# Sums of weights on VectorE alone, kept products in the gated tiles, attention blocks in pairs beside the products, ten masks added by VectorE, and buffers moved by 128 bytes

## The chip, the cores and the metric

The kernel runs on one core of one Trainium2 chip. The metric is the device time of one execution in microseconds (us), as the median of several runs; less is better.

## The reference

It computes windowed attention over eight heads and feeds its output through a gated two-layer network. All data are float32; the inputs q and k are drawn at random and scaled by 0.6244 and 0.6248 in all.

```python
# B=8, H=8, S=576, D=64; d_model=512, d_ff=2048
scores = np.matmul(q, k.transpose(0, 1, 3, 2)) / np.sqrt(D)
rel = pos[:, None] - pos[None, :]
mask_plain = (rel >= 0) & (rel < 32)                          # heads 0-3
mask_dil = (rel >= 0) & (rel < 128) & (rel % 4 == 0)          # heads 4-7
attn = softmax(np.where(masks, scores, -1e9))
x = (attn @ v) arranged as (4608, 512)
h = x @ w_in                                                  # (4608, 2048)
g = h * np.clip(h + 3.0, 0.0, 6.0) / 6.0
out = g @ w_out                                               # (4608, 512)
```

## The kernel before

**Precision.** A float32 matrix product is made of three faster ones: each operand is split into a high part and a low part (value minus high part), and high by high, high by low and low by high are added up in PSUM, the accumulator memory that TensorE writes. So every operand costs a cast (its high part) and a subtraction (its low part) on one of the other engines.

**First phase (up to about 140 us).** A list of steps written out by hand (`ORDER`) starts the attention of the first 12 blocks, converts the weights and runs the first tokens through both layers.

**Planned phase.** Everything after is recorded with `op(engine, cost, ...)` and `transfer(...)` and put in order, engine by engine, by a list scheduler (`_in_time`), which goes by costs written in the code and by counts of free buffers. Each engine then runs its own list strictly in order. Three kinds of work matter here:

- *Plain steps.* Tokens go in chunks of 384, the hidden dimension in 16 slices of 128. A step is the first layer of one slice of one chunk (12 matmuls, L561 to L563, into one of the two banks `ps_h`), then ReLU on ScalarE (L569), the gate on VectorE (L572), its high part by GpSimd (`gh`, L576), its low part by VectorE (`gl`, L580), and two steps later the second layer (9 matmuls, L622). There are 64 of these steps; the bank `ps_h` is free again when the gate has read it.
- *Attention blocks.* `attend` runs a couple: the scores of one block and the values of the block before last, one after the other on TensorE (L237, L255), with softmax on VectorE and ScalarE. The first 20 blocks of the planned phase go in ten pairs of couples beside the plain steps 29 to 56 (`SPOTS`); the other 18 couples stand beside the products of the two groups, where `BESIDE` says (group, k, turn): how many at once. The mask of a block is either one more matmul of TensorE into the scores' bank (L347; the blocks in `PE_MASKS`) or an addition by VectorE, `add_mask` (L263).
- *Two groups.* Most tokens are computed by a scheme of Strassen and Winograd: seven products of sums of blocks in place of eight of blocks. The sums of weights are made once per pair of slices, by `combine(side, k)`: 8 for `w_in` (side 0), 8 for `w_out` (side 1). Each is two word sums (L662, 128x512: high plus low part of a weight), four half sums (L670, 128x256), the high part on ScalarE (L674) and the remainder (L679, 128x1024); two DMAs then write it to DRAM (`sums`, `rights`), from where a ring of six buffers brings it back, 512 KB a piece. The sums of tokens (`fill`, L751 and L758) are VectorE's too, and GpSimd copies pieces of attention output for them (L471). A group's products of one k are 7 times 6 matmuls (L783 to L785), whose results are kept (`keep`, L1081), added (`add`, L1088) and gated (`gated`, L1040 and L1045); then the second layer follows (`second_products`, L774, fed by L1203, L1234, L1238).

Which engine makes the word sums and the remainder is set by the letters in `BY_POOL`: `w` and `l` name GpSimd, `s` (half sums) is not among them, so that these are VectorE's.

Of the kernel before, what the change touches and what calls it, by code (L numbers as in the profile page):

```python
# [9 lines left out]
F32 = mybir.dt.float32  # L10
F32R = mybir.dt.float32r
# [4 lines left out]
AF = mybir.ActivationFunctionType  # L16
# [24 lines left out]
SPOTS = tuple((m, 1) for m in range(29, 57, 3))  # L41
SPARE = (1, 1, 1, 1, 1, 1, 1, 1), (1, 1, 1, 1, 1, 1, 1, 1)
LEAD_SUMS = 300.0
BY_POOL = ("wl",) * 8, ("wl",) * 8
GAPS = {(0, 0): 2}
LATER = 3
LANDING = 2.6
EARLY = 100.0
PE_MASKS = frozenset(range(24))
SHARED = frozenset(range(16))  # L50
WIPED = {(0, 0)}
BESIDE = {**{(0, k, 0): 1 for k in range(8)}, **{(0, k, 3): 1 for k in (2, 4, 6)}, **{(1, k, 0): 1 for k in range(7)}}
HIGH_BY = ("aaaaaaaa",) * 7

# [33 lines left out]
def windowed_attention_ffn(ctx: ExitStack, tc: tile.TileContext, qk, vp, w, mask, out, out_t):  # L88
# [55 lines left out]
    def wide_tile(name, dtype=F32):  # L144
        return work.tile([P, CG], dtype, name=name, tag="work")
# [14 lines left out]
        return mi[:rows, at : at + CH]  # L160

    ident = const.tile([P, P], F32, name="ident")
    three = const.tile([P, 1], F32, name="three")

# [489 lines left out]
    ]  # L654
    KEPT = (T1, T3, T4, T2, R11, R21, R22)

    def combo_words(side, k, i, eng):

        if (side, k) not in combos:
            combos[side, k] = w_tile("v", [4, HALF])  # L660
        x, v = (win, wout)[side][2 * k + i], combos[side, k]
        eng.tensor_tensor(  # L662
            out=v[:, 2 * i : 2 * i + 2].rearrange("p a n -> p (a n)"), in0=x[:, 0].bitcast(F32), in1=x[:, 1].bitcast(F32), op=ALU.add
        )

    def combo_sum(side, k, i, eng):

        v = combos[side, k]
        to, a, b, op = SUMS[side][i]
        eng.tensor_tensor(out=v[:, to], in0=v[:, a], in1=v[:, b], op=op)  # L670

    def combo_high(side, k):
        hi = w_tile("sh", [4, HALF], F32R)
        nc.scalar.copy(hi, combos[side, k])  # L674
        combos[side, k] = combos[side, k], hi

    def combo_low(side, k, i, n, eng):
        v, hi = (x[:, i * 4 // n : (i + 1) * 4 // n] for x in combos[side, k])
        eng.tensor_tensor(out=v.bitcast(F32R), in0=v, in1=hi.bitcast(F32), op=ALU.subtract)  # L679

    def combo_plain(side, k):
        a, b = ((win, wout)[side][2 * k + i] for i in range(2))
# [253 lines left out]
    words, combined, taken = {}, {}, {}  # L936

    def combine(side, k):
        of = lambda what, n: ("POOL", 0.3 + n * 0.00205, nc.gpsimd) if what in BY_POOL[side][k] else ("DVE", 0.16 + n * 0.00104, nc.vector)
        e, us, eng = of("w", DM)  # L940
        x = op(e, us, lambda: combo_words(side, k, 0, eng), takes=[("w", 2, SPARE[side][k])], ahead=LEAD_SUMS)
        words[side, k] = x = op(e, us, lambda: combo_words(side, k, 1, eng), [x], ahead=EVER)
        e, us, eng2 = of("s", HALF)
        for i in range(4):
            x = op(e, us, lambda i=i: combo_sum(side, k, i, eng2), [x], ahead=EVER)
        x = op("ACT", 1.05, lambda: combo_high(side, k), [x], ahead=EVER)
        e, us, eng3 = of("l", 4 * HALF)
        x = op(e, us, lambda: combo_low(side, k, 0, 1, eng3), [x], ahead=EVER)
        combined[side, k] = [
            transfer(0.9, 2.0, lambda: combo_out(side, k), [x], gives=[("w", 2)]),  # L950
            transfer(1.35, 1.5, lambda: combo_plain(side, k), ahead=EARLY),
        ]
# [83 lines left out]
    kept_gates = {}  # L1036

    def gated(h, after, g, q, k, from_bank):
        r = op(
            "ACT", 0.7, lambda: nc.scalar.activation(gated_tile(g, q, k), h(), AF.Relu, bias=three, scale=1.0),  # L1040
            [after, kept_gates.get((g, q, k - 1)) if k % 2 else None], takes=() if k % 2 else SLOT,
        )
        x = op(
            "DVE", 0.69,
            lambda: nc.vector.scalar_tensor_tensor(  # L1045
                out=gated_tile(g, q, k), in0=gated_tile(g, q, k), scalar=6.0, in1=h(), op0=ALU.min, op1=ALU.mult
            ),
            [r], gives=FREE if from_bank else ONE,
        )
        kept_gates[g, q, k] = x  # L1050
        if from_bank:
            freed.append(x)
# [21 lines left out]
    def products_of(g, k):  # L1074

        at_bank, kept = {}, {}

        def keep(name, after):
            def do():
                kept[name] = wide_tile("s")  # L1080
                nc.scalar.copy(kept[name], at_bank["x"])  # L1081

            return op("ACT", 0.59, do, [after], takes=ONE)

        def add(name, bank, after, gives):
            x = op(
# [57 lines left out]
    def second_products(g):  # L1144
# [75 lines left out]
        def halves(p, k):  # L1220
# [7 lines left out]

            def high_():
                two.append(wide_tile("gh", F32R))  # L1230
                if by_pool:
                    nc.gpsimd.tensor_copy(out=two[0], in_=gated_tile(g, q, k))
                else:
                    nc.scalar.copy(two[0], gated_tile(g, q, k))  # L1234

            def low_():
                two.append(wide_tile("gl", F32R))
                nc.vector.tensor_tensor(out=two[1], in0=gated_tile(g, q, k), in1=two[0].bitcast(F32), op=ALU.subtract)  # L1238

            by_pool = HIGH_BY[p][k] == "p"  # L1240
            x = op("POOL" if by_pool else "ACT", 0.8 if by_pool else 0.62, high_, after, takes=[("work", 1, 5)], ahead=8.0)
            y = op("DVE", 0.69, low_, [x], takes=ONE, gives=gives)
            lows[q, name, k] = y
            return two, [x, y]
# [334 lines left out]
```

## Time and profile before

| | |
|---|---|
| median of 3 runs | 862.13 us (862.04 to 862.76) |
| the profiled execution | 861.62 us, of which the span in the profile is 859.8 us |
| TensorE clock granted, mean over the span | 0.988 of full speed |
| busy, share of the span | PE 834.7 us (97%), VectorE 642.9 us (75%), ScalarE 556.8 us (65%), GpSimd 143.5 us (17%) |
| DMA | 184.94 MB in the span, 215 GB/s on the mean |

All views are of this one profiled execution. PE is TensorE's matmul side, PEld its loading of weights; DVE is VectorE, ACT ScalarE, POOL GpSimd, SP the engine that issues DMAs. Busy shares are means over stages with different limits, so the views by stretch of time tell more than this table.

### The profile page before, as it was taken

To read this page: it belongs to the slowest core of one execution; us is meant where nothing else is said; L and a number is where in the kernel's file an instruction comes from. 1 tells how busy PE (TensorE), PEld (TensorE's weight loads), DVE (VectorE), ACT (ScalarE), POOL (GpSimd) and SP (SyncE) were. 2 spreads that over 40 slices of the span, in tenths; PEclk is the share of its full clock that TensorE was granted. 3 is DMA by queue.
4 is the path that set the end of the run, shared out by engine and by line. 5 is a ranking of instruction groups with operands and counts; after the bars stand their busy time and mean duration, and the time that the engine had idled before them with its cause. 6 is when DMAs were issued, how large, how long until landed. Compare 5 with 4: busy or idle time off the path is not lost.

```text
span 859.8 us, 20361 instructions
## 1 busy us (share of the span) xinstructions
PE 834.7 (97%) x8103; PEld 693.8 (81%) x8103; DVE 642.9 (75%) x1130; ACT 556.8 (65%) x1271; POOL 143.5 (17%) x170
## 2 busy tenths in 40 slices
PE   7999999999999889699999999999999999999998
PEld 4788999888888778577778888877888888888886
DVE  4899996567678998976789997566599844449953
ACT  3688776259989786277997774677565524456542
POOL 0000000235447867640011000001000000000000
PEclk9899999999999999889999999999999999999999
DMA  8746433157667879988778475868446369661441
GB/s 299 260 148 232 123 115 129 42 178 238 199 214 247 290 251 349 308 291 278 263 267 287 164 263 168 278 230 301 160 147 227 125 235 378 233 216 55 177 165 74
DMA packets 99454, 184.94 MB, mean 215 GB/s; under 512 B 6560, under 2 KB 35232, under 8 KB 99360
## 3 DMA queue, kind: packets, MB, share of 16 engines
q1 hardware_dynamic: 99360, 183.65, 62.5%
q8 instruction: 64, 1.05, 0.5%
q14 instruction: 30, 0.25, 0.1%
HBM read 144.83 MB, written 38.80 MB: 214 GB/s over the span
## 4 chain that ended last, share of the span: by engine, by line
PE 85%; DVE 9%; ACT 2%; issue 2%; POOL 1%; DMA 1%; SPq 0%; DVEq 0%; POOLq 0%; ACTq 0%
PE ps_o L774 27%; PE ps_o L622 11%; PE ps_x L783 9%; PE ps_x L785 9%; PE ps_x L784 9%; PE ps_h L561 4%; PE ps_h L562 4%; PE ps_h L563 4%; DVE v L670 2%; DVE gl L580 2%; PE ps_b L255 1%; PE ps_a L237 1%; PE ps_a L247 1%; PE ps_a L364 1%; DVE mx L290 1%
## 5 line engine op out<-in xcount | busy, mean ns | idle before, releaser
L774 PE MATMUL ps_o<-gh,ring 128*128 128x512 f32 x672 | 182.7, 389 | 0.0
L774 PEld LDWEIGHTS ps_o<-gh,ring 128*128 128x128 f32 x672 | 126.1, 188 | 26.5
L1238 DVE TENSOR_TENSOR gl<-g,gh 128x512 fp32r<-128x512 f32 x168 | 108.6, 685 | 23.0 <-ACT gh L1234 17.1
L1234 ACT CAST gh<-g 128x512 fp32r<-128x512 f32 x168 | 98.0, 622 | 37.7 <-PE ps_o L774 35.5
L774 PE MATMUL ps_o<-gl,ring 128*128 128x512 f32 x336 | 103.8, 389 | 0.0
L783 PE MATMUL ps_x<-cells,ring 128*128 128x512 f32 x240 | 97.1, 405 | 0.1
L622 PE MATMUL ps_o<-wo,gh 128*128 128x512 f32 x372 | 97.1, 397 | 0.0
L561 PE MATMUL ps_h<-x,wi 128*128 128x384 f32 x256 | 89.5, 350 | 6.2 <-DVE t L572 3.5
L785 PE MATMUL ps_x<-cells,ring 128*128 128x512 f32 x240 | 95.4, 398 | 0.0
L562 PE MATMUL ps_h<-x,wi 128*128 128x384 f32 x256 | 87.3, 341 | 0.6 <-issue 0.6
L563 PE MATMUL ps_h<-x,wi 128*128 128x384 f32 x256 | 87.5, 342 | 0.0
L622 PEld LDWEIGHTS ps_o<-wo,gh 128*128 128x128 f32 x372 | 70.6, 191 | 11.8
L774 PEld LDWEIGHTS ps_o<-gl,ring 128*128 128x128 f32 x336 | 63.1, 188 | 13.3
L784 PE MATMUL ps_x<-cells,ring 128*128 128x512 f32 x176 | 70.0, 398 | 0.0
L580 DVE TENSOR_TENSOR gl<-t,gh 128x384 fp32r<-128x384 f32 x64 | 58.6, 916 | 10.5 <-POOL gh L576 8.5
L1045 DVE SCALAR_TENSOR_TENSOR g<-g,ps_x 128x512 f32<-128x512 f32 x48 | 32.7, 682 | 44.5 <-ACT g L1040 44.0
L784 PE MATMUL ps_x<-cell,ring 128*128 128x512 f32 x160 | 62.8, 392 | 0.0
L471 POOL COPY raw<-xf 128x96 f32<-128x96 f32 (+8 forms) x56 | 23.8, 474 | 221.2 <-ACT xf L402 217.9
L569 ACT ACTIVATE t<-ps_h,three 128x384 f32<-128x384 f32 x64 | 37.3, 585 | 33.9 <-PE ps_h L563 32.0
L402 ACT COPY a<-a_t 32x192 f32<-32x192 f32 x144 | 50.4, 350 | 11.9 <-DVE a L395 7.7
L1203 DVE TENSOR_TENSOR g<-g 128x1024 f32<-128x1024 f32 x48 | 57.4, 1217 | 0.0
L561 PEld LDWEIGHTS ps_h<-x,wi 128*128 128x128 f32 x256 | 48.4, 189 | 10.2 <-DVE t L572 4.5
(129 smaller groups left out, 1699.7 us busy)
## 6 DMA issues: line engine op xcount, KB each, us to landing
ring<-sums SPq DMA_DIRECT2D x84, 512.0 KB, 6.7
ring<-rights SPq DMA_DIRECT2D x84, 512.0 KB, 4.7
st<-in_w SPq DMA_DIRECT2D x32, 512.0 KB, 3.8
kq<-in_qk SPq DMA_DIRECT2D x39, 416.0 KB, 4.0
v<-in_v SPq DMA_DIRECT2D x39, 390.0 KB, 5.3
sums<-wi SPq DMA_DIRECT2D x24, 256.0 KB, 7.2
rights<-wo SPq DMA_DIRECT2D x24, 256.0 KB, 5.4
out<-o SPq DMA_DIRECT2D x11, 512.0 KB, 3.4
```

What stands on the lines that cost most here:

```text
L561: nc.tensor.matmul(ph, lhsT=wt(f, 0)[:, ks], rhs=a, start=(kt == 0), stop=False)
L562: nc.tensor.matmul(ph, lhsT=wt(f, 0)[:, ks], rhs=b, start=False, stop=False)
L563: ins = nc.tensor.matmul(ph, lhsT=wt(f, 1)[:, ks], rhs=a, start=False, stop=(kt == NK - 1))
L580: return nc.vector.tensor_tensor(out=gls[n], in0=ts.pop(n), in1=ghs[n].bitcast(F32), op=ALU.subtract)
L622: ins = nc.tensor.matmul(po[c][tt], lhsT=g[:, tt * P : (tt + 1) * P], rhs=wt(f, row), start=(f == 0 and not i), stop=(f == NF - 1 and i == 2))
L774: nc.tensor.matmul(banks[part], lhsT=right[:, a, cols], rhs=x, start=(start and not i), stop=(i == 2), skip_group_check=True)
L783: nc.tensor.matmul(bank, lhsT=tile_[:, 0, ks], rhs=h[:, kt], start=(start and kt == 0), stop=False, skip_group_check=True)
L784: nc.tensor.matmul(bank, lhsT=tile_[:, 0, ks], rhs=l[:, kt], start=False, stop=False, skip_group_check=True)
L785: nc.tensor.matmul(bank, lhsT=tile_[:, 1, ks], rhs=h[:, kt], start=False, stop=(kt == 1), skip_group_check=True)
L1203: nc.vector.tensor_tensor(out=at[0], in0=at[1], in1=at[2], op=alu)
L1234: nc.scalar.copy(two[0], gated_tile(g, q, k))
L1238: nc.vector.tensor_tensor(out=two[1], in0=gated_tile(g, q, k), in1=two[0].bitcast(F32), op=ALU.subtract)
```

## The change

It has six parts. (1) `BY_POOL` goes: the 32 word sums and the 16 remainders are VectorE's, as the half sums were. (2) `keep` writes a product into the gated tile of its slice, which lies in the pool of 4 KB slots, in place of a work tile; the ReLU of a kept product writes a work tile in its turn. (3) `BESIDE` puts single couples and pairs beside the products, where there were single ones only: 11 beside the first group and 7 beside the second, as before. (4) Ten blocks (0 to 9 of the planned phase) get their mask from VectorE rather than from TensorE. (5) Two more slices of the first group clear a bank by a matmul (L1105) before a product is copied into it, so that the bank is taken earlier. (6) The tile `three` takes 160 bytes a partition where it took 4, and everything allocated behind it lies 128 bytes higher. `HIGH_BY` named ScalarE throughout; it goes, and nothing is moved by that.

```diff
-BY_POOL = ("wl",) * 8, ("wl",) * 8
-PE_MASKS = frozenset(range(24))
+PE_MASKS = frozenset(range(10, 24))
-WIPED = {(0, 0)}
-BESIDE = {**{(0, k, 0): 1 for k in range(8)}, **{(0, k, 3): 1 for k in (2, 4, 6)}, **{(1, k, 0): 1 for k in range(7)}}
-HIGH_BY = ("aaaaaaaa",) * 7
+WIPED = {(0, 0), (0, 6), (0, 7)}
+BESIDE = {**{(0, k, 0): 1 for k in range(3)}, **{(0, k, 0): 2 for k in range(3, 7)}, (1, 0, 0): 1, **{(1, k, 0): 2 for k in (2, 4, 6)}}
...
-    three = const.tile([P, 1], F32, name="three")
+    three = const.tile([P, 40], F32, name="three")[:, :1]
...
     def combine(side, k):
-        of = lambda what, n: ("POOL", 0.3 + n * 0.00205, nc.gpsimd) if what in BY_POOL[side][k] else ("DVE", 0.16 + n * 0.00104, nc.vector)
-        e, us, eng = of("w", DM)
-        x = op(e, us, lambda: combo_words(side, k, 0, eng), takes=[("w", 2, SPARE[side][k])], ahead=LEAD_SUMS)
-        words[side, k] = x = op(e, us, lambda: combo_words(side, k, 1, eng), [x], ahead=EVER)
-        e, us, eng2 = of("s", HALF)
+        x = op("DVE", 0.69, lambda: combo_words(side, k, 0), takes=[("w", 2, SPARE[side][k])], ahead=LEAD_SUMS)
+        words[side, k] = x = op("DVE", 0.69, lambda: combo_words(side, k, 1), [x], ahead=EVER)
         for i in range(4):
-            x = op(e, us, lambda i=i: combo_sum(side, k, i, eng2), [x], ahead=EVER)
+            x = op("DVE", 0.43, lambda i=i: combo_sum(side, k, i), [x], ahead=EVER)
         x = op("ACT", 1.05, lambda: combo_high(side, k), [x], ahead=EVER)
-        e, us, eng3 = of("l", 4 * HALF)
-        x = op(e, us, lambda: combo_low(side, k, 0, 1, eng3), [x], ahead=EVER)
+        x = op("DVE", 1.22, lambda: combo_low(side, k), [x], ahead=EVER)
...
     def gated(h, after, g, q, k, from_bank):
+        t = {}
+
+        def do():
+            t[0] = gated_tile(g, q, k) if from_bank else wide_tile("t")
+            nc.scalar.activation(t[0], h(), AF.Relu, bias=three, scale=1.0)
...
-                out=gated_tile(g, q, k), in0=gated_tile(g, q, k), scalar=6.0, in1=h(), op0=ALU.min, op1=ALU.mult
+                out=gated_tile(g, q, k), in0=t[0], scalar=6.0, in1=h(), op0=ALU.min, op1=ALU.mult
...
         def keep(name, after):
...
-                kept[name] = wide_tile("s")
+                kept[name] = gated_tile(g, q, k)
                 nc.scalar.copy(kept[name], at_bank["x"])
 
-            return op("ACT", 0.59, do, [after], takes=ONE)
+            return op("ACT", 0.59, do, [after, kept_gates.get((g, q, k - 1)) if k % 2 else None], takes=() if k % 2 else SLOT)
```

The lines of the changed kernel have other numbers: the gate L572 is L570 there, `gl` L580 is L578, a token sum L751 or L758 is L749 or L756, a word sum L662 is L660, a half sum L670 is L668, a remainder L679 is L677, GpSimd's cast L576 is L574 and its copies L471 are L469.

The first place is GpSimd's list around the last casts of gates, up to the cast of the 64th, which is the last L576. Before, sums of weights stand between the casts (`wo` is a weight of the second layer, `v` and `sh` a sum and its high part):

```order
L576 CAST gh<-t 128x384
L662 TENSOR_TENSOR v<-wo 128x512
L679 TENSOR_TENSOR v<-v,sh 128x1024
L576 CAST gh<-t 128x384
L662 TENSOR_TENSOR v<-wo 128x512 x3
L576 CAST gh<-t 128x384 x2
L679 TENSOR_TENSOR v<-v,sh 128x1024 x2
L576 CAST gh<-t 128x384
L679 TENSOR_TENSOR v<-v,sh 128x1024 x2
```

With the change the same stretch of GpSimd's list, up to the same last cast, holds copies of attention output and casts:

```order
L574 CAST gh<-t 128x384
L469 COPY raw<-xf 128x2x48
L469 COPY raws<-xf 128x2x64
L469 COPY raw<-xf 128x2x80
L574 CAST gh<-t 128x384 x6
```

All sums are gone from between the casts; nothing takes their place on GpSimd.

The second place is VectorE's list around the same gates, from the 61st to the low part of the 64th. Before, half sums and token sums (`cells`, `cell`) stand between gate and low part:

```order
L572 SCALAR_TENSOR_TENSOR t<-t,ps_h 128x384
L670 TENSOR_TENSOR v<-v 128x256 x5
L580 TENSOR_TENSOR gl<-t,gh 128x384
L670 TENSOR_TENSOR v<-v 128x256
L572 SCALAR_TENSOR_TENSOR t<-t,ps_h 128x384
L670 TENSOR_TENSOR v<-v 128x256 x2
L580 TENSOR_TENSOR gl<-t,gh 128x384
L670 TENSOR_TENSOR v<-v 128x256 x6
L758 TENSOR_TENSOR cell<-raws,cells 128x1024
L572 SCALAR_TENSOR_TENSOR t<-t,ps_h 128x384
L758 TENSOR_TENSOR cells<-t,cells 128x1024
L580 TENSOR_TENSOR gl<-t,gh 128x384
```

With the change the same stretch reads:

```order
L570 SCALAR_TENSOR_TENSOR t<-t,ps_h 128x384
L756 TENSOR_TENSOR cells<-t,cells 128x1024
L578 TENSOR_TENSOR gl<-t,gh 128x384
L660 TENSOR_TENSOR v<-wo 128x512
L668 TENSOR_TENSOR v<-v 128x256
L660 TENSOR_TENSOR v<-wo 128x512
L570 SCALAR_TENSOR_TENSOR t<-t,ps_h 128x384
L668 TENSOR_TENSOR v<-v 128x256
L677 TENSOR_TENSOR v<-v,sh 128x1024
L578 TENSOR_TENSOR gl<-t,gh 128x384
L668 TENSOR_TENSOR v<-v 128x256 x4
L756 TENSOR_TENSOR cell<-raws,cells 128x1024
```

Word sums and remainders have come between the gates, and half sums have left them: over VectorE's list from the 51st to the 64th gate there are 20 half sums, 10 word sums and 5 remainders where there were 35 half sums. From the 28th to the 51st gate there are 14 word sums, 5 remainders and 10 masks more and 2 half sums fewer; from the 64th gate to the first low part of the second layer (L1238) 8 word sums, 6 remainders and 18 half sums where there was one half sum. These three stretches hold all 32 word sums and 16 remainders.

The third place is VectorE's list beside the first group, where `BESIDE` puts couples (`e` is a score tile with its mask added, `mx` the rows' largest scores, `z` their sums; the numbers tell buffers apart). Before, one couple stood there at a time:

```order
L263 TENSOR_TENSOR e_6153<-ps_b_6092,mi_81 128x384
L322 TENSOR_SCALAR z_6161<-ps_b_6093 128x6
L323 RECIPROCAL z_6161<-z_6161 128x6
L325 TENSOR_TENSOR x_6164<-ps_b_6093,z_6161 128x384
L289 TENSOR_REDUCE mx_6175<-e_6153 128x6
L290 TENSOR_SCALAR mx_6175<-mx_6175 128x6
L1045 SCALAR_TENSOR_TENSOR g_6157<-g_6157,s_5525 128x512
```

With the change, where a pair stands:

```order
L261 TENSOR_TENSOR e_6167<-ps_b_6041,mi_81 128x384
L261 TENSOR_TENSOR e_6174<-ps_a_6091,mi_81 128x384
L287 TENSOR_REDUCE mx_6188<-e_6167 128x6
L288 TENSOR_SCALAR mx_6188<-mx_6188 128x6
L287 TENSOR_REDUCE mx_6193<-e_6174 128x6
L288 TENSOR_SCALAR mx_6193<-mx_6193 128x6
L320 TENSOR_SCALAR z_6204<-ps_a_6092 128x6
L321 RECIPROCAL z_6204<-z_6204 128x6
L323 TENSOR_TENSOR x_6207<-ps_a_6092,z_6204 128x384
```

The masks and maxima of two blocks now stand together, ahead of the next product's gate, where those of one block did.

## Rows read from the trace of the kernel before

**Rows 1.** Windows: us of window, PE, PEld, DVE, ACT, POOL busy (instructions), PEclk, DMA, GB/s.

```profile
166.00:280.00 114.00, 114.00 (x1786) 99.88 (x1788) 80.88 (x178) 93.47 (x300) 56.43 (x65) 1.00 0.63 205
280.00:365.00 85.00, 70.30 (x839) 60.19 (x828) 79.91 (x119) 51.89 (x138) 60.40 (x53) 0.95 0.90 301
280.00:380.00 100.00, 85.28 (x1070) 71.87 (x1059) 91.93 (x134) 61.65 (x161) 68.14 (x57) 0.93 0.89 295
365.00:455.00 90.00, 89.90 (x1371) 70.95 (x1372) 68.94 (x147) 75.39 (x192) 15.11 (x26) 0.97 0.82 275
720.00:740.00 20.00, 20.00 (x88) 16.16 (x87) 7.93 (x12) 9.19 (x16) 0.00 (x0) 1.00 1.05 386
```

**Rows 2.** Waits of PEld, 280 to 380 us: total us, times, longest.

```profile
PEld ps_b L255 <- DVE t L572: 4.7, 1, 4.7
PEld ps_h L561 <- DVE t L572: 4.5, 3, 2.6
PEld ps_h L561 <- ACT e L298: 3.4, 2, 3.2
PEld ps_a L255 <- ACT o L922: 2.5, 1, 2.5
```

**Rows 3.** The chain within 340 to 366 us, by line.

```profile
by line: DVE v L670 27.2%; DVE gl L580 19.0%; DVE cell L758 17.8%; POOL gh L576 13.2%; DVE cells L758 8.5%; issue 8.4%; DVE t L572 7.2%; DVE t L751 4.4%; DVEq L580 0.2%; POOLq L576 0.1%; DVEq L572 0.1%
```

**Rows 4.** VectorE's groups, 280 to 365 us: busy us, mean ns, idle before.

```profile
L580 DVE TENSOR_TENSOR gl<-t,gh 128x384 fp32r<-128x384 f32 x13 | 20.0, 1541 | 1.4 <-POOL gh L576 1.4
L670 DVE TENSOR_TENSOR v<-v 128x256 f32<-128x256 f32 x35 | 19.9, 598 | 0.3
L290 DVE TENSOR_SCALAR mx<-mx 128x6 f32<-128x6 f32 x6 | 7.3, 1213 | 0.2
...
L758 DVE TENSOR_TENSOR cell<-t,cells 128x1024 fp32r<-128x1024 f32 x1 | 3.4, 3405 | 0.0
```

**Rows 5.** VectorE's groups, 60 to 140 us, when GpSimd was idle.

```profile
L580 DVE TENSOR_TENSOR gl<-t,gh 128x384 fp32r<-128x384 f32 x21 | 11.6, 552 | 0.1
...
L545 DVE TENSOR_TENSOR wo<-va,wo 128x512 fp32r<-128x512 f32 x13 | 8.9, 686 | 1.2 <-ACT wo L539 1.1
```

**Rows 6.** GpSimd's groups, 280 to 365 us.

```profile
L662 POOL TENSOR_TENSOR v<-wo 128x512 f32<-128x512 f32 x16 | 23.1, 1458 | 0.0
L679 POOL TENSOR_TENSOR v<-v,sh 128x1024 fp32r<-128x1024 f32 x8 | 20.1, 2521 | 1.1 <-ACT sh L674 1.1
L576 POOL CAST gh<-t 128x384 fp32r<-128x384 f32 x13 | 10.2, 785 | 20.8 <-DVE t L572 20.8
L471 POOL COPY raws<-xf 128x128 f32<-128x128 f32 (+4 forms) x10 | 5.5, 551 | 0.0
L471 POOL COPY raw<-xf 128x160 f32<-128x160 f32 (+3 forms) x6 | 3.7, 610 | 0.0
```

**Rows 7.** Timeline, 304 to 305 us: start us, us.

```profile
304.08 2.38 POOL L679 TENSOR_TENSOR v<-v,sh 128x1024 fp32r<-128x1024 f32 x1
304.25 2.23 DVE L290 TENSOR_SCALAR mx<-mx 128x6 f32<-128x6 f32 x1
```

**Rows 8.** VectorE's groups over the whole span.

```profile
L1203 DVE TENSOR_TENSOR g<-g 128x1024 f32<-128x1024 f32 x48 | 57.4, 1217 | 0.0
...
L263 DVE TENSOR_TENSOR e<-ps_b,mi 128x384 f32<-128x384 f32 x12 | 6.6, 550 | 2.3 <-PE ps_b L237 2.3
```

**Rows 9.** TensorE's timeline around a couple with a mask of TensorE's.

```profile
398.21 0.40 PE L785 MATMUL ps_x<-cells,ring 128*128 128x512 f32 x1
398.44 0.34 PE L347 MATMUL ps_b<-mi 128*128 128x384 bf16 x1
398.71 0.24 PE L255 MATMUL ps_b<-v,a 64*32 64x65 f32 x1
```

**Rows 10.** TensorE's timeline around a couple without such a mask.

```profile
413.73 0.39 PE L785 MATMUL ps_x<-cell,ring 128*128 128x512 f32 x1
414.05 0.24 PE L255 MATMUL ps_b<-v,a 64*32 64x65 f32 x1
```

More of the change, by code (lines that the diff above doesn't have):

```diff
@@ L655, in windowed_attention_ffn, with combo_words @@
     KEPT = (T1, T3, T4, T2, R11, R21, R22)
-    def combo_words(side, k, i, eng):
+    def combo_words(side, k, i):
         if (side, k) not in combos:
@@ L661, in combo_words, with combo_sum @@
         x, v = (win, wout)[side][2 * k + i], combos[side, k]
-        eng.tensor_tensor(
+        nc.vector.tensor_tensor(
             out=v[:, 2 * i : 2 * i + 2].rearrange("p a n -> p (a n)"), in0=x[:, 0].bitcast(F32), in1=x[:, 1].bitcast(F32), op=ALU.add
         )
-    def combo_sum(side, k, i, eng):
+    def combo_sum(side, k, i):
         v = combos[side, k]
         to, a, b, op = SUMS[side][i]
-        eng.tensor_tensor(out=v[:, to], in0=v[:, a], in1=v[:, b], op=op)
+        nc.vector.tensor_tensor(out=v[:, to], in0=v[:, a], in1=v[:, b], op=op)
     def combo_high(side, k):
@@ L675, in combo_high, with combo_low @@
         combos[side, k] = combos[side, k], hi
-    def combo_low(side, k, i, n, eng):
-        v, hi = (x[:, i * 4 // n : (i + 1) * 4 // n] for x in combos[side, k])
-        eng.tensor_tensor(out=v.bitcast(F32R), in0=v, in1=hi.bitcast(F32), op=ALU.subtract)
+    def combo_low(side, k):
+        v, hi = combos[side, k]
+        nc.vector.tensor_tensor(out=v.bitcast(F32R), in0=v, in1=hi.bitcast(F32), op=ALU.subtract)
     def combo_plain(side, k):
@@ L1038, in gated @@
     def gated(h, after, g, q, k, from_bank):
+        t = {}
+        def do():
+            t[0] = gated_tile(g, q, k) if from_bank else wide_tile("t")
+            nc.scalar.activation(t[0], h(), AF.Relu, bias=three, scale=1.0)
         r = op(
-            "ACT", 0.7, lambda: nc.scalar.activation(gated_tile(g, q, k), h(), AF.Relu, bias=three, scale=1.0),
-            [after, kept_gates.get((g, q, k - 1)) if k % 2 else None], takes=() if k % 2 else SLOT,
+            "ACT", 0.7, do, [after, kept_gates.get((g, q, k - 1)) if k % 2 else None],
+            takes=ONE if not from_bank else () if k % 2 else SLOT,
         )
@@ L1078, in keep @@
         def keep(name, after):
+            q = int(name[1:])
             def do():
-                kept[name] = wide_tile("s")
+                kept[name] = gated_tile(g, q, k)
                 nc.scalar.copy(kept[name], at_bank["x"])
-            return op("ACT", 0.59, do, [after], takes=ONE)
+            return op("ACT", 0.59, do, [after, kept_gates.get((g, q, k - 1)) if k % 2 else None], takes=() if k % 2 else SLOT)
         def add(name, bank, after, gives):
@@ L1230, in high_ @@
                 two.append(wide_tile("gh", F32R))
[L1231 to L1234, printed above, removed]
+                nc.scalar.copy(two[0], gated_tile(g, q, k))
             def low_():
@@ L1238, in low_ @@
                 nc.vector.tensor_tensor(out=two[1], in0=gated_tile(g, q, k), in1=two[0].bitcast(F32), op=ALU.subtract)
-            by_pool = HIGH_BY[p][k] == "p"
-            x = op("POOL" if by_pool else "ACT", 0.8 if by_pool else 0.62, high_, after, takes=[("work", 1, 5)], ahead=8.0)
+            x = op("ACT", 0.62, high_, after, takes=[("work", 1, 5)], ahead=8.0)
             y = op("DVE", 0.69, low_, [x], takes=ONE, gives=gives)
```

## The prediction

> **What bounds the kernel now.** The windows view comes first: busy time of each engine by stretch [rows 1]. From 166 to 280 us TensorE's matmul side is busy for 114.00 of 114 us at the full clock, and from 365 to 455 us for 89.90 of 90: there nothing but fewer matmuls shortens the run. Between 280 and 380 us it is busy for 85.28 of 100 us and its granted clock is 0.93. The first is 14.7 us of idleness; the second is 7.0 us more (100 x 0.07), since the matmuls that do run are drawn out when the clock falls to its lower level (1.2 in place of 2.4 GHz) in part of a stretch that has gaps. These 21.7 us are what a better order could give back.
>
> Who holds TensorE up there the list of waits tells [rows 2]: 4.7 and 4.5 us for the gate L572, 3.4 and 2.5 us for the exponentials and for a scaled output on ScalarE, 15.1 us together. Three of the four end at softmax or gate work, which comes off VectorE's list or behind it. The chain of waits from 340 to 366 us names the cause more sharply [rows 3]: half sums L670 27%, low parts L580 19%, token sums L758 26%, gates 7%, all VectorE's, and 13% GpSimd's cast. In the windows VectorE is busy for 79.91 of the 85 us from 280 to 365 [rows 1]. So VectorE is full exactly where TensorE starves.
>
> But is it full of work? In that stretch one L580 takes 1541 ns on the mean, one L670 598, one L290 (128x6 elements!) 1213, one token sum 3405 [rows 4]. From 60 to 140 us, with GpSimd idle, the same L580 takes 552 ns, and a 128x512 addition 686 [rows 5]; a 128x1024 one takes 1217 [rows 8]. From these two a 128x256 half sum would take 0.42 us (0.686 less half of 0.531). The excess is 13 x 0.99 = 12.9 us in L580, 35 x 0.18 = 6.3 in L670, 6 x about 1.0 = 6 in L290 (an estimate: 64 times the elements take 0.55 in L263 [rows 8]), 2.2 in that one L758: some 27 us of records that are blocked, not working. What blocks them is seen in the timeline: GpSimd's remainder starts at 304.08 and lasts 2.38 us, L290 starts at 304.25 and lasts 2.23, both end at 306.46 to 306.48 [rows 7]. GpSimd is busy there for 60.40 us [rows 1], of which word sums and remainders are 23.1 + 20.1 = 43.2 and the casts and copies 19.4 [rows 6].
>
> **Part 1, the sums to VectorE.** *Added work:* 32 word sums at 0.686 us and 16 remainders at 1.217 [rows 5, 8], 22.0 + 19.5 = 41.4 us, with the ten masks at 0.55 (5.5 us) 46.9. By VectorE's order it falls in three places.
> - From the 28th to the 51st gate, about 166 to 280 us: 14 x 0.686 + 5 x 1.217 + 10 x 0.55 - 2 x 0.42 = 20.3 us. VectorE's 80.88 of 114 us [rows 1] become at most 101. It stays hidden behind matmuls that are unbroken now; without that cover it would cost its 20.3 us.
> - From the 51st to the 64th gate: 10 x 0.686 + 5 x 1.217 - 15 x 0.42 = 6.6 us.
> - From the 64th gate to the first low part of the second layer: 8 x 0.686 + 6 x 1.217 + 17 x 0.42 = 19.9 us. VectorE's 68.94 of 90 us [rows 1] become 88.8.
>
> *Removed:* GpSimd's 43.2 us in the starved stretch. VectorE's 91.93 busy us from 280 to 380 hold about 27 of blocking, so 64.5 of work; with 6.6 more 71.1. What GpSimd keeps there, 19.4 us of casts and copies, is 0.32 of its 60.40; if blocking goes with GpSimd's time, 27 x 0.32 = 8.7 us stay: 79.8 us of VectorE against 78.3 of TensorE at the full clock (100 - 21.7). That is 1.5 us over, on par. The bounds of what TensorE still loses there are 0 and today's 14.7. I take 3.5: the 1.5, and 2 for gates whose cast or low part stands behind a 1.2 us sum in a full queue. Beside the first group I take 3.5 as well: 88.8 us in a window of some 88 leaves VectorE no slack, but a few us of the 68.94 were blocking by GpSimd's last remainders. Bounds there: nothing, and the whole 19.9 if VectorE's idle time of before (21 of 90 us) can't be used because results it waits for come late. With gaps this short I let the clock come back whole; a clock that stays low keeps up to 7.0.
>
> By the order, GpSimd's casts now stand behind no sum on their own engine. That shortens the way from gate to low part only where a sum ran when the gate ended: GpSimd was idle for 20.8 us ahead of casts, until their gate came [rows 6]. I count nothing for it beyond the unblocking.
>
> The pair of records at 304 us shows whole instructions waiting for one another [rows 7]. The Trainium skill says why, in "SBUF — State Buffer", section "SBUF: two separate sides": VectorE and GpSimd share a pair of ports, held as an exclusive lock for a whole instruction, and a VectorE operation with two SBUF inputs contends with a GpSimd operation that reads SBUF. The trace agrees for the two-input L580, but the proportional 8.7 us would be too mild by that rule: it is what the third case below prices.
>
> **Part 2, kept products in the gated tiles.** The copies, additions and gates keep their sizes and engines; nothing is added. What changes is which pool they wait for: the 4 KB slots are taken at the copy rather than at the ReLU. In rows of before no wait there names either pool; I take 0, with bounds of 2 us either way.
>
> **Part 3, pairs beside the products.** TensorE's entry into a couple costs 0.32 us from the last product matmul (413.73 to 414.05) where the next matmul otherwise follows after 0.23 (398.21 to 398.44) [rows 9, 10]: 0.09 per entry. Seven couples join another; the way back to the products isn't in these rows, and I take it alike: 0.7 us gained, between 0 and 1.3. In VectorE's list two masks and two maxima now stand ahead of a product's gate, about 1.8 us more delay there (0.55 + 0.55 and smaller ones); six banks for products and scores hide it, and it is in the 3.5 above.
>
> **Part 4, ten masks.** With TensorE's mask the block's first matmul comes 0.50 us after the last product (398.21 to 398.71), without it 0.32 [rows 9, 10]: 0.18 each, 1.8 us gained for ten, in stretches where TensorE is unbroken. Bounds: 0 and 3.4 (ten times the record's 0.34). VectorE's side is counted above.
>
> **Part 5, two wipes:** two 128x512 matmuls at the products' pitch of 0.23, 0.5 us lost. **Part 6, 128 bytes:** no instruction changes its size; I take 0, bounds 2 us either way: DMA's busy share is 0.89 in the starved stretch [rows 1], but none of the waits there ends with a DMA [rows 2].
>
> **The sum**, against the profiled execution's own 861.6 us (span 859.8 and 1.8 around it): - 21.7 - 0.7 - 1.8 + 0.5 + 3.5 + 3.5 = 844.9. The median of the runs lies 0.5 above the profiled one, so 845.4.
>
> **Rivals.**
> - *All stalls go* (VectorE's sums fit between the gates, casts come early): neither 3.5 is paid, 838.4. For it: VectorE would be on par even with blocking that stays. Against: par leaves no room for a bad order.
> - *Half the gain* (each cast and copy blocks VectorE for its whole length): 19.4 in place of 8.7 stay, 10.7 us more on a VectorE that is the bound: 845.4 + 10.7 = 856. For it: the pair of records at 304 us [rows 7]. Against: some casts run while VectorE waits for that very cast (1.4 us idle before L580 [rows 4]), and such a cast blocks nothing.
> - *DMA late.* By the order of SP's list twelve pieces of sums for `w_out`, about 0.52 MB each, move past the 64th gate, into the window that carries 275 GB/s for 90 us = 24.8 MB [rows 1]. About 31 MB in 88 us are 352 GB/s; 386 is the most in any of these windows. If ring pieces come behind these writes, some 10 us: 855. Against: TensorE's waits name no DMA in rows 2.
> - *Slower: VectorE becomes the bound.* If the excess of 27 us isn't GpSimd's sums (it could come with DMA or PSUM traffic), it stays: 91.9 + 6.6 = 98.5 us of VectorE against 78.3, a stall of 20, and its clock loss of 7 stays; beside the first group half of the 19.9, 10 us, come out on the path. 838.4 + 20 + 7 + 10 = 875. It decides from 23.7 us of stalls and clock loss on (21.7 + 0.7 + 1.8 - 0.5). Against: the common end at 306.46, and 552 ns in rows 5 under other DMA and PSUM traffic.
>
> **The numbers.** Forecast (841 to 850): 0.42. All stalls go: 0.20. Half the gain: 0.20. DMA: 0.06. VectorE the bound: 0.12. The range of 8 in 10 leaves out the last and the ends of the others: 836 to 857. About 0.2% (1.7 us) can be told from no change; faster by more 0.86, same 0.03, slower 0.11.
>
> **What would show it.** Right: no L662 or L679 on GpSimd, L580 near 0.6 to 0.8 us and half sums near 0.42 between 280 and 365 us; TensorE busy for over 93 of 100 us there and its clock back near 1.00; waits on gates under 5 us. Wrong: L580 still above 1.2 us (blocking not by the sums); PEld waiting for L1045 or L1091 beside the first group for over 5 us (VectorE full there); waits of products that end with a DMA.

## The result, and the profile after

The changed kernel takes 849.1 us (median of four runs, 847.94 to 849.82) where the kernel before takes 862.44 beside it: a ratio of 0.9838, with an interval of 0.9819 to 0.9856. The profiled execution takes 849.62 us, 12.0 us less than that of before; its span is 847.4 us. A second measurement of the same kernel (`again`, below) gives 0.9821 (0.9794 to 0.9848).

The page's lines for TensorE's and GpSimd's busy time, and for the shares of the chain that ended last:

```profile
PE 827.2 (98%) x8095; PEld 691.7 (82%) x8095; DVE 639.2 (75%) x1188; ACT 557.4 (66%) x1271; POOL 59.3 (7%) x122
...
PE 89%; ACT 4%; DMA 2%; DVE 2%; issue 2%; POOL 0%; SPq 0%; DVEq 0%; ACTq 0%; POOLq 0%
```

VectorE has taken over 41 us of sums and is still busy for 3.7 us less than before (642.9): its records have become shorter. The windows by stretch, columns as in [rows 1]:

```profile
166.00:280.00 114.00, 112.11 (x1914) 99.89 (x1913) 86.72 (x204) 97.56 (x305) 26.20 (x49) 1.00 0.63 205
280.00:380.00 100.00, 99.83 (x1285) 85.58 (x1284) 89.54 (x183) 70.95 (x184) 16.95 (x26) 0.99 0.96 326
342.00:440.00 98.00, 92.43 (x1387) 73.02 (x1386) 82.38 (x181) 79.19 (x196) 10.41 (x26) 0.98 0.90 314
365.00:455.00 90.00, 84.39 (x1169) 66.32 (x1168) 74.12 (x158) 77.97 (x194) 10.20 (x26) 0.98 0.87 309
530.00:620.00 90.00, 88.22 (x825) 70.99 (x824) 57.42 (x108) 60.60 (x133) 4.81 (x14) 0.98 0.64 227
```

The starved stretch is gone: from 280 to 380 us TensorE is busy for 99.83 of 100 us, where it was 85.28 [rows 1]. But it is now idle for 1.9 us ahead of it, 5.6 us beside the first group (365 to 455) and 1.8 us beside the second (530 to 620), and those three were full before (90.00 of 90 us in the last). The first of them isn't new, though. It is the wait for a scaled output at 278 us, and the kernel before has the same wait inside the starved stretch (start, us, line, idle before):

```profile
283.30 0.24 PE L255 MATMUL ps_a<-v,a 64*32 64x65 f32 x1 [2.26 <-ACT o L922]
```

The windows are fixed in time and the work in them has moved ahead, so that this wait has left the stretch without going away. (The trace has three groups of products, not two; couples stand beside the first two, and the third has none.) VectorE's groups from 265 to 350 us, where the last plain steps now run:

```profile
L668 DVE TENSOR_TENSOR v<-v 128x256 f32<-128x256 f32 x28 | 11.9, 446 | 0.2
L578 DVE TENSOR_TENSOR gl<-t,gh 128x384 fp32r<-128x384 f32 x16 | 8.9, 554 | 2.0 <-POOL gh L574 2.0
```

The low part of a gate takes 554 ns where it took 1541, a half sum 446 where it took 598 [rows 4]. The waits of TensorE's matmuls from 160 to 830 us (total us, times, longest):

```profile
PE ps_x L782 <- issue: 3.4, 1, 3.4
PE ps_x L781 <- ACT g L1084: 2.1, 2, 1.5
PE ps_a L253 <- ACT o L920: 1.9, 1, 1.9
PE ps_a L253 <- issue: 1.8, 1, 1.8
PE ps_o L620 <- issue: 0.2, 1, 0.2
```

No wait for a gate is left, and no wait for VectorE at all. Two end with ScalarE: for a scaled output (L920) and for kept copies (L1084). The two longest other ones are called "issue": TensorE waited for nothing that the profile shows. What that is, the experiments had to tell.

### The profile page after: what moved, and what is told of

Same layout as the page of the kernel before. It is cut to its first block, busy times and chain, and to the rows that moved or that the text cites. A ratio compares the mean times of both kernels' runs of the same rounds, so it can differ in the third digit from the quotient of the medians.

```text
span 847.4 us, 20299 instructions
## 1 busy us (share of the span) xinstructions
PE 827.2 (98%) x8095; PEld 691.7 (82%) x8095; DVE 639.2 (75%) x1188; ACT 557.4 (66%) x1271; POOL 59.3 (7%) x122
## 4 chain that ended last, share of the span: by engine, by line
PE 89%; ACT 4%; DMA 2%; DVE 2%; issue 2%; POOL 0%; SPq 0%; DVEq 0%; ACTq 0%; POOLq 0%
PE ps_o L772 27%; PE ps_o L620 14%; PE ps_x L781 9%; PE ps_x L782 8%; PE ps_x L783 8%; PE ps_h L559 5%; PE ps_h L560 5%; PE ps_h L561 5%; PE ps_a L235 2%; PE ps_a L253 2%; DMA kq<-in_qk 1%; PE ps_a L362 1%; PE ps_a L245 1%; PE ps_b L253 1%; ACT a L400 1%
## 5 line engine op out<-in xcount | busy, mean ns | idle before, releaser
L1238 DVE TENSOR_TENSOR gl<-g,gh 128x512 fp32r<-128x512 f32 x168 | 108.8, 687 | 24.7 <-ACT gh L1234 18.3
L620 PE MATMUL ps_o<-wo,gh 128*128 128x512 f32 x372 | 94.6, 390 | 0.2 <-issue 0.2
L782 PE MATMUL ps_x<-cells,ring 128*128 128x512 f32 x176 | 70.3, 399 | 3.4 <-issue 3.4
L782 PE MATMUL ps_x<-cell,ring 128*128 128x512 f32 x160 | 63.6, 397 | 0.0
L1091 DVE TENSOR_TENSOR g<-ps_x,g 128x512 f32<-128x512 f32 x48 | 33.1, 689 | 39.8 <-ACT g L1084 32.7
L783 PEld LDWEIGHTS ps_x<-cells,ring 128*128 128x128 f32 x240 | 45.9, 191 | 14.7 <-issue 3.6
L781 PEld LDWEIGHTS ps_x<-cells,ring 128*128 128x128 f32 x240 | 45.8, 191 | 12.3 <-ACT g L1084 0.8
L620 PE MATMUL ps_o<-wo,gl 128*128 128x512 f32 x186 | 52.2, 389 | 0.0
L400 ACT COPY a<-a_t 32x192 f32<-32x192 f32 x144 | 50.5, 350 | 2.6
```

The lines of the kernel that those rows point to most:

```text
L400: ins = nc.scalar.copy(dst[QB * to : QB * (to + 1), u * CH // 2 : (u + 1) * CH // 2], mid[QB * c : QB * (c + 1), : CH // 2])
L620: ins = nc.tensor.matmul(po[c][tt], lhsT=g[:, tt * P : (tt + 1) * P], rhs=wt(f, row), start=(f == 0 and not i), stop=(f == NF - 1 and i == 2))
L781: nc.tensor.matmul(bank, lhsT=tile_[:, 0, ks], rhs=h[:, kt], start=(start and kt == 0), stop=False, skip_group_check=True)
L782: nc.tensor.matmul(bank, lhsT=tile_[:, 0, ks], rhs=l[:, kt], start=False, stop=False, skip_group_check=True)
L783: nc.tensor.matmul(bank, lhsT=tile_[:, 1, ks], rhs=h[:, kt], start=False, stop=(kt == 1), skip_group_check=True)
```

## The experiments

All of them run the whole computation; only the two with fillings and `shift` add work that nothing uses.

**Is it GpSimd's sums?** Two kernels separate the first part from the rest. `pool_back` is the changed kernel with the sums on GpSimd again:

```diff
 def combo_words(side, k, i):
-        nc.vector.tensor_tensor(
+        nc.gpsimd.tensor_tensor(
 def combo_low(side, k):
-        nc.vector.tensor_tensor(out=v.bitcast(F32R), in0=v, in1=hi.bitcast(F32), op=ALU.subtract)
+        nc.gpsimd.tensor_tensor(out=v.bitcast(F32R), in0=v, in1=hi.bitcast(F32), op=ALU.subtract)
```

with the three operations recorded for GpSimd at the former costs.

> The changed kernel with its 32 word sums and 16 remainders on GpSimd again; all else as changed. Theory 1 (GpSimd's sums block VectorE's records, and VectorE then starves TensorE): the stalls return, 858 to 863 us, one gl subtraction (128x384) over 1.2 us on the mean between 280 and 360 us. Rival (the gain came from the pairs, the masks and the kept products): the time stays under 853.

`only_sums` is the kernel before with nothing but the first part:

```diff
-BY_POOL = ("wl",) * 8, ("wl",) * 8
+BY_POOL = ("",) * 8, ("",) * 8
```

> The kernel before with nothing changed but the sums, all on VectorE. Theory 1: almost the whole gain, 846 to 851 us, gl near 0.56 us. Rival (the other parts carry the gain, or they make the room that the sums need): 856 or more.

`pool_back` takes 864.28 us, a ratio of 1.0022 (1.0005 to 1.0038): without the first part the other five gain nothing. VectorE's groups from 265 to 350 us and TensorE's waits in its profile:

```profile
L668 DVE TENSOR_TENSOR v<-v 128x256 f32<-128x256 f32 x32 | 23.2, 743 | 0.4 <-POOL v L660 0.2
L578 DVE TENSOR_TENSOR gl<-t,gh 128x384 fp32r<-128x384 f32 x13 | 15.5, 1195 | 1.1 <-POOL gh L574 1.1
```

```profile
PE ps_b L253 <- DVE t L570: 6.4, 1, 6.4
PE ps_h L559 <- DVE t L570: 6.1, 5, 4.0
```

The low part takes more than twice as long as in the changed kernel, the half sum 1.7 times as long, and TensorE waits 12.5 us for gates again. Two details of the expectation were missed: the time is 1.3 us above its range, and between 280 and 360 us, the window that was set, the low part takes 1076 ns, not over 1200. `only_sums` takes 853.42 us, 0.9879 (0.9853 to 0.9904): most of the gain, but some 4 us short of the whole and above the expected 851. Its low parts take 552 ns. Its waits:

```profile
PE ps_b L255 <- DVE x L325: 4.3, 1, 4.3
PE ps_x L783 <- issue: 2.3, 1, 2.3
PE ps_b L237 <- ACT e L298: 2.2, 1, 2.2
PE ps_h L562 <- issue: 2.0, 2, 1.3
```

The first stands at 390 us, beside the first group, and the chain ahead of it runs through two remainders (L679, 1.23 and 1.13 us) that stand among VectorE's softmax operations. That is the wait that the forecast's second 3.5 us stood for.

**Is it blocking, or the casts that queue behind the sums?** Both would fit so far. Two kernels put fillings on GpSimd behind each pair's word sums, on a buffer of their own; the lists of the other four engines stay the same, instruction for instruction.

```diff
+        for _ in range(4):
+            op("POOL", 0.0, lambda: [nc.gpsimd.tensor_tensor(out=beside_it, in0=beside_it, in1=beside_it, op=ALU.add) for _ in range(2)], [x], ahead=EVER)
```

and `nc.gpsimd.memset(beside_it, 0.0)`, three times, in the other.

> The changed kernel with 128 additions (128x128, on a buffer that nothing else uses) put on GpSimd behind the weight sums, which stay on VectorE; the lists of the four other engines are the same, instruction for instruction. Theory 1 (records of VectorE are blocked while GpSimd reads SBUF): gl and the sums on VectorE grow, by 10 to 25 us in all, and the time is 853 to 862. Rival (blocking is not it; GpSimd's sums only delayed the casts queued behind them): gl stays at 0.55 us, and the time is that of the next kernel, whose fillings delay the casts alike.

> As the kernel with additions, but GpSimd writes zeros (192 fills of 128x128, no reading) in their place. Theory 1: VectorE's records stay at their free length (gl 0.55 to 0.6 us) and the time within 3 us of the changed kernel's 849. Rival (any GpSimd work in front of the casts costs the time): as long as the kernel with additions, to 2 us.

With additions 853.7 us, 0.9877 (0.9841 to 0.9914); with fills 846.35, 0.9799 (0.9777 to 0.9822), no slower than the changed kernel. VectorE's groups from 265 to 350 us, with additions and then with fills:

```profile
L670 DVE TENSOR_TENSOR v<-v 128x256 f32<-128x256 f32 x25 | 11.9, 498 | 0.1
L580 DVE TENSOR_TENSOR gl<-t,gh 128x384 fp32r<-128x384 f32 x16 | 9.8, 613 | 8.2 <-POOL gh L576 8.2
L662 DVE TENSOR_TENSOR v<-wo 128x512 f32<-128x512 f32 x9 | 7.2, 804 | 0.0
```

```profile
L670 DVE TENSOR_TENSOR v<-v 128x256 f32<-128x256 f32 x28 | 11.7, 441 | 0.2
L580 DVE TENSOR_TENSOR gl<-t,gh 128x384 fp32r<-128x384 f32 x16 | 8.9, 559 | 3.1 <-POOL gh L576 3.1
L662 DVE TENSOR_TENSOR v<-wo 128x512 f32<-128x512 f32 x12 | 8.3, 689 | 0.0
```

GpSimd's groups of fillings in the same stretch:

```profile
L942 POOL TENSOR_TENSOR beside_it<-beside_it 128x128 f32<-128x128 f32 x58 | 32.5, 561 | 4.0
```

```profile
L942 POOL MEMSET beside_it<- 128x128 f32 x109 | 22.3, 204 | 5.9
```

The fills keep GpSimd busy for 22.3 us and lengthen nothing; the additions lengthen VectorE's sums, remainders and low parts, the word sum by 115 ns, but not the gate, one of whose two operands is in PSUM (534 against 537 ns). The records that overlap, from 140 to 460 us, say the same from GpSimd's side: a fill takes 205 ns on the mean beside an operation of VectorE with both inputs in SBUF, the on-chip memory, and 206 ns otherwise; an addition takes 602 and 408 ns. So reading is what blocks. That agrees with the Trainium skill ("SBUF — State Buffer", section "SBUF: two separate sides"): a two-input VectorE operation contends with a GpSimd operation that reads SBUF, not with one that only writes it. The size is under what was expected: VectorE is busy for 647.3 us with additions and for 639.1 with fills, 8.2 us more and not 10 to 25. About 4.4 of them lie in this stretch (count by lengthening, over these three groups, the remainders at 1423 against 1276 ns, and the other word sums at 764 against 677).

The 7 us between the two times aren't a measure of the blocking. With additions one wait of TensorE's ends with a gate:

```profile
PE ps_b L255 <- DVE t L572: 1.3, 1, 1.3
```

All its waits from 160 to 830 us are 14.4 us with additions and 8.9 with fills, and 3.0 of the 5.5 between are of the kind called "issue". The two didn't load GpSimd alike either: the idle time ahead of low parts, ended by a cast, is 8.2 us with additions and 3.1 with fills. So these two kernels show what lengthens VectorE's records; that lengthened records cost TensorE its time rests on `pool_back` and `only_sums`. A late cast can be little of that: in the kernel before and in `pool_back` the idle time ahead of low parts that a cast ends is 1.4 us [rows 4] and 1.1 us.

**What are the waits without a releaser?** A couple is 96 matmuls and 96 loads of weights, 0.96 us from its first to its last matmul where nothing breaks it. The page's third part shows a queue of instructions (queue and kind: packets, MB, share of 16 engines):

```profile
q8 instruction: 64, 1.05, 0.5%
```

That is 64 packets of 16 KB in the span, one for about 253 of TensorE's 16,190 instructions; by this count the queue is TensorE's. A pair of couples runs through one and a half such packets in some 2 us. Around the wait in front of L782 (from 381.2 to 384.6 us) the DMA view of the changed kernel has these lines:

```profile
q1 hardware_dynamic: 847, 1.26, 104.4%
q8 instruction: 1, 0.02, 1.8%
```

While TensorE stands still one packet of instructions comes in, on engines that are full of data. Four kernels follow: the changed one again, and the couples one at a time as before, everywhere or beside one of the groups.

```diff
-BESIDE = {**{(0, k, 0): 1 for k in range(3)}, **{(0, k, 0): 2 for k in range(3, 7)}, (1, 0, 0): 1, **{(1, k, 0): 2 for k in (2, 4, 6)}}
+BESIDE = {**{(0, k, 0): 1 for k in range(8)}, **{(0, k, 3): 1 for k in (2, 4, 6)}, **{(1, k, 0): 1 for k in range(7)}}
```

(`single`; `single0` takes only the entries with a leading 0 from the second line, `single1` only those with a leading 1.)

> The changed kernel once more, for its own spread and for a second profile. Theory A (TensorE's two waits without a releaser, 3.4 us at 381 and 1.9 us at 567, come with the pairs beside the products): both stand in this profile too, at the same places in the program. Rival (chance events of one execution): they are elsewhere or gone, and the time is near 846. Expected 849.

> The changed kernel with the couples beside the products one at a time, where the kernel before had them. Theory A (pairs cost TensorE waits for its own instructions, and put the kept copies behind two blocks' exponentials on ScalarE): waits without a releaser under 1 us in all, 844 to 846 us. Rival (the sum of the forecast: pairs gain 0.7): 850.

> Single couples beside the first group only; pairs stay beside the second. Theory A: the wait of 3.4 us in the first group and the clock's drop behind it go, and most of the 3 us that TensorE waits for ScalarE's copies; 845 to 847. The 1.9 us in the second group stay. Rival: 849 to 850.

> Single couples beside the second group only; pairs stay beside the first. Theory A: the wait of 1.9 us and the clock's drop behind it go, 846 to 847.5 us, and the 3.4 us in the first group stay. Rival: 849 to 850.

`again`: 847.66 us; its profile has the same two waits, 3.9 us in front of the same L782 and 2.1 in front of the same L253. They are no chance events. `single`: 844.04 us, 0.9785 (0.9753 to 0.9818), with single runs from 840.81 to 849.38. `single0`: 845.24 us, 0.9792 (0.9765 to 0.9819). `single1`: 847.09 us, 0.9815 (0.9788 to 0.9841). The intervals overlap that of `again`; only the medians say that one at a time is better. The waits in the profile of `single`:

```profile
PE ps_a L253 <- ACT o L920: 1.9, 1, 1.9
PE ps_x L781 <- ACT g L1084: 1.1, 1, 1.1
PE ps_b L235 <- ACT e L296: 1.0, 1, 1.0
PE ps_o L620 <- issue: 0.7, 2, 0.4
```

Both long waits are gone there, at a span of 839.0 us; but this profile is of the shortest of its six runs, and what the longer ones waited for isn't known. `single1` has lost the second (and keeps 3.6 us of the first), as expected. But `single0` has kept 2.8 us in front of its L782 with single couples there, where `single`, with the same list of TensorE up to the second group, has none. So pairs aren't the cause by themselves: the theory stood for the second group and fell for the first. The packet itself tells the two apart: in `single` it comes in at 377.3 us, some 100 matmuls ahead of that place; in `single0`, as in the changed kernel, `again` and `single1`, it comes in only when TensorE already stands still there. Why it is late in these four, no run shows.

What is left is the place of the packets' borders. `shift` moves nothing but these: 64 small matmuls at the very start, 128 instructions, half a packet.

```diff
+    for _ in range(64):
+        nc.tensor.matmul(idle[:, :32], lhsT=zeros[:, :P], rhs=zeros[:, P : P + 32], start=True, stop=True)
```

> The changed kernel with 64 more small matmuls (128x32 of zeros) ahead of everything on TensorE, so that every later instruction stands 128 instructions further along in TensorE's program; the other engines' lists and the rest of TensorE's are the same. Theory A (the two waits without a releaser are TensorE waiting for a 16 KB page of its own program, which is late where couples run through instructions fast while data DMAs fill the engines): the waits at 385 and 568 us move to other instructions or go. Rival (something at those very instructions makes them wait): they stay at the same instructions, with the same length to 0.5 us.

It takes 874.21 us, 1.0107 (1.0068 to 1.0146): slower than the kernel before. Its runs lie at 866.55 to 868.38 (three) and at 874.21 to 877.03 (four), and the profile is of one of 868.19, with a span 18.6 us longer than the changed kernel's. The plain steps start 3.1 us later for the added matmuls; the rest is this, in TensorE's waits from 160 to 830 us:

```profile
PE ps_a L256 <- issue: 13.3, 7, 4.1
PE ps_a L238 <- issue: 7.9, 5, 1.9
PE ps_a L256 <- ACT o L923: 1.9, 1, 1.9
```

The wait in front of the product is gone, and there are twelve in front of attention matmuls, first among them (start, us, line, idle before):

```profile
193.23 0.24 PE L256 MATMUL ps_a<-v,a 64*32 64x65 f32 x1 [3.18 <-issue]
```

Between 190 and 193 us a packet of instructions comes in there too. The waits follow the border, not the instruction: TensorE waits for its own program. All profiles together bear this out. They have 44 waits of over 0.4 us called "issue" after 140 us, and 43 of them end 1.2 to 1.6 us after a packet of this queue has landed; the one that does not is in `single_o`, below. What makes the longer four runs of `shift` 6 us longer, no profile shows. How long a wait is, the windows around three of them tell (columns as in [rows 1]; the waits in them are 3.2, 1.5 and 4.1 us):

```profile
189.00:193.00 4.00, 1.05 (x92) 0.88 (x79) 0.92 (x4) 0.52 (x2) 0.00 (x0) 1.00 1.03 329
208.00:212.00 4.00, 2.46 (x193) 2.21 (x190) 0.83 (x2) 3.27 (x7) 1.95 (x2) 1.00 0.35 111
...
410.00:415.00 5.00, 0.86 (x90) 0.70 (x77) 1.94 (x5) 3.37 (x8) 1.01 (x2) 1.00 1.08 379
```

Where DMA's share is 0.35 to 0.71 the waits are 1.1 to 1.9 us (seven more in this profile are of this kind), in the two windows here where it is over 1 they are 3.2 and 4.1 us; one of 0.7 us, at 398 us, stands in full DMA too. The page of the Trainium skill on this ("Runtime: NRT & Kernel Launch", section "Instruction fetch mechanics") has blocks of 16 KiB for 256 instructions, as here, and calls the cost of passing a border mostly hidden; here it is hidden in plain steps by themselves (42 instructions in 4.1 us) and not where couples stand or have just ended.

**The masks and the small parts.** `masks` has `PE_MASKS = frozenset(range(24))` again. `rest_back` takes back parts 2, 5 and 6: `keep` and `gated` as before, `WIPED = {(0, 0)}`, and `three` as a tile of `[P, 1]`.

> The changed kernel with the ten masks by TensorE again. The forecast's term: 1.8 us slower, 849 to 851. Rival (with VectorE as full as it is, its 5.5 us of masks cost as much as TensorE saves): the same as the changed kernel, 847 to 849.

> The changed kernel without its three small parts: products kept in work tiles, one wipe, and buffers where they were (128 bytes lower). The forecast's terms: within 2 us of the changed kernel's 848. Rival (one of them carries a part of the gain): 851 or more.

`masks` takes 855.53 us, 0.9908 (0.9879 to 0.9938), slower than either theory had it. In its plain steps the masks cost a little more than was forecast: from the first matmul of a step with a pair to that of the next it takes up to 0.58 us more than in the changed kernel (6.88 against 6.40 in one of them), 2.2 us over the five such steps, 0.22 a mask. The rest is in the waits:

```profile
PE ps_a L253 <- issue: 6.3, 2, 4.6
PE ps_h L560 <- issue: 3.1, 2, 1.8
```

9.4 us for the program where the changed kernel has 5.4: ten masks are 20 instructions, and every border behind them has moved. `rest_back` takes 856.26 us, 0.9918 (0.9888 to 0.9947), not within 2 us of the changed kernel. Two causes show in its profile. The first is a wait of 5.1 us beside the first group, at 401 us, for ScalarE's copies (L400); the program's, 5.3 us in all, are about as long as in the changed kernel (5.4):

```profile
PE ps_b L253 <- ACT a L400: 5.4, 2, 5.1
PE ps_x L782 <- issue: 3.1, 1, 3.1
PE ps_a L235 <- issue: 2.2, 1, 2.2
```

The second is in every plain step. The first matmul of two steps that follow each other, in the kernel before, in the changed one and in `rest_back`:

```profile
163.43 0.34 PE L561 MATMUL ps_h<-x,wi 128*128 128x384 f32 x1
...
167.63 0.34 PE L561 MATMUL ps_h<-x,wi 128*128 128x384 f32 x1
```

```profile
162.66 0.34 PE L559 MATMUL ps_h<-x,wi 128*128 128x384 f32 x1
...
166.79 0.34 PE L559 MATMUL ps_h<-x,wi 128*128 128x384 f32 x1
```

```profile
165.17 0.34 PE L559 MATMUL ps_h<-x,wi 128*128 128x384 f32 x1
...
169.37 0.34 PE L559 MATMUL ps_h<-x,wi 128*128 128x384 f32 x1
```

The same 21 matmuls take 4.20, 4.13 and 4.20 us. `only_sums` has 4.20 too; `again`, `single`, `masks` and `shift`, which keep part 6, have 4.13. So have the other profiles with part 6, eleven in all. Parts 2 and 5 touch only operations of the groups, far behind these steps; what differs in them is the address of the buffers. That is argued: no run moves the addresses and nothing else.

**A wait on ScalarE.** `single_o` is `single` with the scaled outputs of the plain steps on VectorE (`put_out` with `("DVE",)`).

> Couples one at a time, as in the fastest kernel so far, and the scaled outputs of the plain steps by VectorE rather than by ScalarE. If the 1.9 us wait at 278 us (blocks waiting for a scaled output on ScalarE) is ScalarE's queue, it goes with the clock's drop behind it: 840 to 842.5 us. Rival (VectorE is full there too, and is late in its turn): 844 to 848.

847.2 us, 0.9815 (0.9784 to 0.9846): no better than `single`, and within the rival's range. At the same place TensorE now waits 2.4 us, and the page calls that wait "issue":

```profile
279.03 0.68 DVE L922 TENSOR_SCALAR o<-ps_o 128x512 f32<-128x512 f32 x1
...
279.81 0.28 PE L253 MATMUL ps_a<-v,a 64*32 64x65 f32 x1 [2.40 <-issue]
```

This one isn't the program's: the last packet of instructions had landed 9.0 us before. VectorE's scaled output ends at 279.71 us, 0.1 us ahead of the matmul, as ScalarE's does in `single` (278.25 and 278.30). So the matmul still waits for the scaled output, which is now late on VectorE, behind half sums and a low part: the rival.

## Why the prediction was right, point by point

849.1 us lie in the range, 3.7 above the 845.4. The steps:

- *The bound.* Right. GpSimd's sums blocked VectorE, whose gates starved TensorE; `pool_back` brings it back, `only_sums` takes it away, and the two kernels with fillings show that reading by GpSimd is enough to lengthen VectorE's records. Of the signs set, the low part came out under its band (554 ns for 600 to 800); TensorE is busy for 99.83 of 100 us, the clock is 0.99, and no wait for a gate is left.
- *What stays there (3.5 us).* Right in size by luck: 3.8 us. They are 0.2 of idleness, 1.9 for the scaled output, now at 278 us, and 1.7 of clock behind it (0.57 from 279 to 283 us). The sum counted this wait, the 2.5 us of L922 in [rows 2], among those that go with VectorE's blocking, without a reason; it stays in every kernel here, between 1.2 and 2.5 us. The step that gave the 3.5, blocking in proportion to GpSimd's remaining time (8.7 us), was too much. Casts and copies do block (from 140 to 460 us a cast takes 840 ns beside a two-input operation and 508 otherwise), but only seven of VectorE's 85 two-input records between 280 and 380 are over 60 ns longer than such records are alone, by 1.6 us in all (before 28 of 60, by 25.8). The low part is none of them (554 ns against 552 in [rows 5]): it waits for its own cast. The case that counted all casts and copies against VectorE (half the gain) is out.
- *Beside the first group (3.5 us).* 5.6 us idle and 1.7 of clock, and the cause was wrong: VectorE isn't full. The stretch of the forecast, from the 64th gate to the first low part of the second layer, is now 342 to 440 us; VectorE is busy for 82.38 of 98 us there, where the forecast had 88.8 of some 88, and no wait of TensorE's ends with it. 3.4 us are the program's and 2.1 ScalarE's kept copies. Where VectorE's sums are among softmax without part 2, in `only_sums`, the forecast wait does stand, 4.3 us; that part 2 took it away is argued from `rest_back` and not shown alone.
- *Not in the sum at all:* the waits for the program, the 3.4 us above and 1.8 us beside the second group with 1.7 of clock. "The clock comes back whole" failed with them: three of the four longest waits, at 278, 385 and 568 us, are each followed by a stretch at 1.2 GHz; from 385 to 389 us the granted clock is 0.58.
- *The masks (1.8 us).* Nearly right in size: 0.22 each, 2.2 for ten.
- *The pairs (0.7 us gained).* Right where it can be read: beside the second group, from its first product matmul to its last, single couples take 96.1 us (before, `single`, `single1`) and pairs 95.6 to 95.8 without their waits and clock loss (the changed kernel, `again`, `single0`), 0.3 to 0.5 us for three entries. By the medians single couples are faster all the same: what a pair gains at its entry is less than what a late packet costs.
- *DMA late.* Out for the data: no wait of TensorE's ends with a piece. But the window of the 3.4 us for the program, 380 to 385 us, has a DMA share of 1.06.
- *The 128 bytes (0, bounds 2 us).* Mis-sized: 0.07 us a plain step, about 4.5 us for 64, a gain, if the address is the cause. No row of before shows another address.

Profile against profile: - 21.7, + 3.8 that stay of them, + 7.3 and + 3.5 beside the two groups, - 2.2 masks, - 0.5 pairs, + 0.5 wipes, - 4.5 pitch make - 13.8; measured are - 12.0. The 1.8 us between aren't assigned. So the cause and the main size, the starved stretch, were forecast, but the number came as close as it did by luck, because errors of opposite sign met: some 7 us more loss beside the two groups than the sum had, some 5 us more gain from the pitch and the masks.

Open stays which of parts 2 and 5 carries the rest of `rest_back`'s loss, and why a packet of the program comes in late in one kernel and in time in another with the same list up to there.

## What to carry to other kernels

When an engine is full in a starved stretch, compare its records there with the same operation elsewhere: records that were two or three times as long were another engine's doing here, and moving that engine's work over can add instructions and lower the busy time. Before a difference of a few us between two versions is put down to the edit, look at the waits without a releaser, at whether a packet of instructions landed just before each ended, and at the pitch of untouched loops: the place of every later instruction and of every buffer has moved as well. Where TensorE runs through many small matmuls, the borders of its program can be a cost of their own, which no count of work shows.

## What the runs showed of the hardware that was not expected

- TensorE waited up to 4.6 us for a 16 KB packet of its own program where couples (192 instructions in about 1 us) stand, and went on 1.2 to 1.6 us after the packet had landed; 128 added instructions at the start raised these waits from 5.4 to 21.2 us and the ratio to the kernel before from 0.9838 to 1.0107. Those of `shift` were 1.1 to 1.9 us at a DMA share of 0.35 to 0.71, and 3.2 and 4.1 us, but also 0.7, where it was over 1.
- An untouched plain step of 21 matmuls takes 4.13 us in the eleven profiles with all buffers 128 bytes higher and 4.20 in the three without. Why, and whether the address alone does it, no run here shows.
- Fills on GpSimd (204 ns each) left VectorE's records alone; additions on GpSimd lengthened them by 54 to 147 ns.
